# Transposing k and q by DMA and holding attention back, in a kernel that fuses attention with a two-layer MLP

## The chip, the cores and the metric

The kernel runs on one core of a Trainium2 chip. The core has a matrix engine (TensorE, PE in the profile, with its weight loads as PEld), a vector engine (DVE), an activation engine (ACT), GpSimd (POOL) and SyncE (SP), which here issues all DMAs. The metric is the device time of one execution in microseconds: 277.5 us before, the median of three runs (277.43 to 278.24).

## The reference

Eight batches of attention with 8 heads, 576 positions and 64 values per head. First 32 packed queries p per head attend over k and v; then the positions q attend over the 32 packed results. The output, 4608 tokens of 512 values, goes through an MLP with 2048 hidden values and a swish with a slope for each hidden value. All inputs and the output are float32.

```python
p_packed = sm_attn(p, k, v)                 # softmax(p k^T / 8) v
out = sm_attn(q, p_packed, p_packed)        # softmax(q pp^T / 8) pp
x = out.transpose(0, 2, 1, 3).reshape(4608, 512)
h = x @ w_in
g = h * (1 / (1 + exp(-beta * h)))
return g @ w_out
```

## The kernel before

The kernel works in bf16 with float32 sums. It goes batch by batch through four stages. Each head's 576 positions are split into a main part of 512 and a remainder of 64.

**Loads.** SP loads k, q and v of a batch as float32 (`plan_loads`, issues at L214 for the main part and L222 for the remainder, two DMAs), POOL casts them into one bf16 tile of 128 x 2304 each (L242, L248; DVE for the main part of batch 0). There is one float32 tile and one bf16 tile for each of k, q and v, so the load of the next batch waits for the cast, and the cast for the last reader of the bf16 tile (`readers`, L258).

**Transposes.** TensorE transposes k and q of each batch: four groups of eight 128x128 blocks (`transpose`, L270, two groups each), and four blocks for the remainders of both (`transpose_rest`, L300). DVE copies the results from PSUM to SBUF (`evacuate`, L277; `evacuate_rest`, L310), into one tile for k (kT, with kTr for the remainder) and one for q (qT).

**Attention.** The first scores `s1` and `s1r` (L332, L348) multiply the transposed k with p; ACT takes the exponentials; `z1` sums them, `pun` multiplies with v (the packing product, L395, tile pp_ps), `pp` normalizes. The second scores `s2` (L430) multiply the transposed q with pp; ACT exponentials, sums `z2`, and on ACT a logarithm and an exponential give the reciprocal; DVE makes the weights A2 (L480). Since the second attention and W1 are both linear in pp, the product of pp and w_in is made first (`fused_w`, L525) and scaled with beta by DVE (`scaled_w`, tile W, L537).

**MLP.** W1 (`h`, L562) multiplies W with A2 in 16 pieces of two matmuls of 512 columns, ACT takes silu into g_main (L570). `hr` does it for the remainder. W2 (`o`, L620) multiplies g_main with w_out: four token groups t of 16 matmuls each (64 a batch), summed in one PSUM bank a group; the remainders of two batches make one more group of 16 (g_rem). DVE copies a group's result to o_sb (three tiles, L629), SP stores it (L637, L641).

**What sets the order.** All this is written as tasks with an engine, an estimated duration, dependencies and a rank (`task`, L190). `Planner.run` (L63) simulates the engines with these durations and emits the instructions of each engine in the order in which the simulated engines start them: a free engine takes the ready task with the lowest rank. W1 of batch b has rank 100b - 300, its attention 100b - 30 and above, loads 100b, W2 100b + 260: so W2 fills in where nothing else is ready. On the chip each engine runs its instructions in this fixed order and waits for semaphores. PSUM is planned as three rings: two banks for h, two for o, four ("att") for the rest. ACT has one table of functions for exp and ln and another for silu; the planner decides when it changes (L109 to L118). Before 36 us it fills a free TensorE with dummy matmuls (L120, warm_ps).

W1 of batch b waits for the whole of W2 of batch b-2 (`oldg`, L599), since g_main has two buffers; A2 and W of batch b wait for W1 of batch b-2.

Of the kernel before, what the change touches and what calls it, by code (L numbers as in the profile page):

```python
# [29 lines left out]
LAND_US = 2.0  # L30
WARM_UNTIL = 36.0
WN = 1


class Task:

    __slots__ = ("engine", "us", "fn", "deps", "rank", "takes", "count", "ends", "table", "end", "slot", "left", "ready", "users", "key")

    def __init__(self, engine, us, fn, deps, rank, takes, count, ends, table):
# [4 lines left out]
        self.left, self.ready = 0, 0.0  # L46


class Planner:
# [8 lines left out]
    def add(self, engine, us, fn, deps=(), rank=0, takes=None, count=1, ends=(), table=None):  # L58
        t = Task(engine, us, fn, [d for d in deps if d is not None], rank, takes, count, ends, table)
        self.tasks.append(t)  # L60
        return t

    def run(self):  # L63
# [72 lines left out]
class Kernel:  # L136
# [128 lines left out]
    def plan_attention(self, b):  # L265
# [10 lines left out]

        def evacuate(x, i, engine):  # L277
            if i == 0:
                st[b, x, "T"] = self.tr.tile(
                    [128, NC, S if x == "q" else SM], bf16, tag=f"{x}T", name=f"{x}T"  # L280
                )
            self.copy[engine](  # L282
                st[b, x, "T"][:, 2 * i : 2 * i + 2, 0:SM],
                st[b, x, "ps", i][:].rearrange("p (c n) -> p c n", c=2),
            )

        for x in "kq":
            old = [("s1", b - 1, i) for i in range(2)] if x == "k" else [("s2", b - 1, i) for i in range(2)]
            for i in range(2):
                tr = self.task(  # L290
                    ("tr", b, x, i), "PE", 0.45, lambda x=x, i=i: transpose(x, i),
# [16 lines left out]
                    )  # L308

        def evacuate_rest(x):  # L310
            ps = st[b, "r", "ps"]
            if x == "k":
                st[b, "kr"] = t = self.tr.tile([128, 2, 128], bf16, tag="kTr", name="kTr")
                nc.vector.tensor_copy(t[:], ps[:, 0:256].rearrange("p (u n) -> p u n", u=2))
            else:
                nc.vector.tensor_copy(
                    st[b, "q", "T"][:, :, SM:S].rearrange("p (g u) n -> p u g n", u=2),
                    ps[:, 256:512].rearrange("p (u g n) -> p u g n", u=2, g=2),
                )

        trr = self.task(
            ("trr", b), "PE", 0.24, transpose_rest,
            [("cast", b, "k", 2), ("cast", b, "q", 2), ("s1r", b - 1), ("T", b, "q", 1)], rank + 1, takes="att",
        )
        rk = self.task(("rk", b), "DVE", 0.28, lambda: evacuate_rest("k"), [trr], rank + 1)
        self.task(("rq", b), "DVE", 0.28, lambda: evacuate_rest("q"), [trr, rk], rank + 1, ends=[trr])


        E = lambda: self.E1T[b % 2]
# [18 lines left out]
        def scores1_rest():  # L348
            st[b, "s1r"] = ps = self.att("s1r_ps")
            for u in range(2):  # L350
                self.mm(
                    ps[:, 0:256].rearrange("p (g u e) -> p u g e", g=2, u=2)[:, u],
                    st[b, "kr"][:, u, :],
                    pT().rearrange("p (g u) e -> p u g e", u=2)[:, u],
                )

# [70 lines left out]
        self.task(("pp", b), "DVE", 0.6, normalize1, [i1, pun], rank + 4, ends=[pun])  # L427


        def scores2(name, lo, hi):  # L430
            for r in range(2):
                st[b, name, r] = self.att(name + "_ps")
            for c in range(NC):
                for r in range(2):
                    self.mm(
                        st[b, name, r][32 * c : 32 * c + 32, 0 : hi - lo],
                        st[b, "pp"][64 * r : 64 * r + 64, c, :],
                        st[b, "q", "T"][64 * r : 64 * r + 64, c, lo:hi],
                        pos=(64 * r, 32 * c),
                    )  # L440

# [38 lines left out]
        def weights2(i):  # L480
# [17 lines left out]
        s2r = self.task(  # L498
            ("s2", b, 1), "PE", 0.14, lambda: scores2("s2r", SM, S),
            [("pp", b), ("rq", b), s2] + oldE, rank + 5, takes="att", count=2,  # L500
        )
        e2r = [
# [366 lines left out]
```

## Time and profile before

| what | value |
|---|---|
| median of three runs | 277.5 us |
| the profiled execution, as a whole | 278.71 us |
| its span, first to last instruction | 276.8 us |
| mean granted TensorE clock | 0.991 |
| HBM read and written | 37.23 MB and 9.44 MB |
| changes of ACT's table | 32, 41.1 us |
| DVE waiting for W2's results before copying them | 83.2 us |

The profile was taken from one execution. Times within it start at its first instruction. A group row gives line, engine, operation, output and inputs with shapes, count, then busy time and mean ns of one, then idle time of the engine just before them and what ended most of it. Matmuls are pipelined, their ends are modelled and overlap the next ones, so the distance between starts says how long an instruction holds the engine in a full queue. In rows of the timeline the brackets hold the idle time before and what ended it. The DMA queue of SP appears as SPq.

### The profile page before, as it was taken

What the parts mean: (1) busy time and instruction counts of PE and PEld (TensorE: products, weight loads), DVE (VectorE), ACT (ScalarE), POOL (GpSimd) and SP (SyncE); (2) the same over time, 40 slices, a digit from 0 to 9 for tenths busy, and PEclk for the clock granted to TensorE, in tenths of its full rate; (3) what the DMA queues carried; (4) which work ended last, traced back from release to release, by engine and by line L of the source; (5) the groups of instructions that cost most, each with busy time, mean ns of one, the idle gap of its engine ahead of it and who ended that gap; (6) DMA issues with size and microseconds to landing.
All of it is one profiled execution on the core that took longest, in us unless ns stands there. A gap on an engine that the chain in (4) does not pass through costs nothing.

```text
span 276.8 us, 5707 instructions
## 1 busy us (share of the span) xinstructions
PE 260.0 (94%) x2394; PEld 138.7 (50%) x2394; DVE 131.8 (48%) x232; ACT 173.0 (62%) x296; POOL 60.6 (22%) x58
## 2 busy tenths in 40 slices
PE   4998687979999999999999999999999999999993
PEld 4995254535555444654365434564355444454441
DVE  6645744798239635823752374224681373021120
ACT  1457458695988798588867984678648875630000
POOL 4107633060444630063005400044000000000000
PEclk9999998899999999999999999999999999999999
DMA  6999999958999999208920793000200110111112
GB/s 208 294 344 357 315 288 370 341 175 232 290 295 313 276 284 287 57 0 252 334 83 0 225 336 108 22 18 38 78 38 15 49 54 38 38 40 76 76 76 76
DMA packets 47736, 47.02 MB, mean 170 GB/s; under 512 B 14288, under 2 KB 38880, under 8 KB 47712
## 3 DMA queue, kind: packets, MB, share of 16 engines
q1 hardware_dynamic: 47712, 46.68, 56.2%
q8 instruction: 18, 0.29, 0.5%
q14 instruction: 6, 0.05, 0.1%
HBM read 37.23 MB, written 9.44 MB: 169 GB/s over the span
## 4 chain that ended last, share of the span: by engine, by line
PE 86%; DVE 5%; DMA 3%; ACT 2%; SPq 1%; issue 0%; POOL 0%; POOLq 0%; DVEq 0%
PE o_ps L167 45%; PE h_ps L167 18%; PE w_ps L167 3%; DMA w_out<-in_moe_w_out_dram 3%; PE hr_ps L167 3%; PE kT_ps L172 2%; PE qT_ps L172 2%; PE z_ps L167 2%; PE warm_ps L167 2%; PE s_ps L167 2%; DVE A2T L483 2%; PE pp_ps L167 2%; PE brow_ps L167 2%; SPq L222 1%; DVE W_bf L542 1%; DVE identr L672 1%
## 5 line engine op out<-in xcount | busy, mean ns | idle before, releaser
L167 PE MATMUL o_ps<-w_out_bf,g_main 128*128 128x512 bf16 x512 | 125.6, 381 | 3.8 <-DVE w_out_bf L791 2.0
L573 ACT ACTIVATE g_main<-h_ps 128x512 bf16<-128x512 f32 x128 | 71.2, 595 | 46.5 <-PE h_ps L167 46.0
L167 PEld LDWEIGHTS <-g_main 128*128 128x128 bf16 x512 | 46.9, 98 | 57.2 <-issue 8.5
L167 PE MATMUL h_ps<-A2T,W_bf 128*128 128x512 bf16 x256 | 69.9, 381 | 1.2 <-DVE W_bf L542 1.1
L631 DVE COPY o_sb<-o_ps 128x512 f32<-128x512 f32 x36 | 24.8, 690 | 83.3 <-PE o_ps L167 83.2
L167 PEld LDWEIGHTS <-W_bf 128*128 128x128 bf16 x512 | 32.0, 98 | 27.4 <-issue 3.9
L542 DVE TENSOR_TENSOR W_bf<-w_ps,beta_bc 128x512 bf16<-128x512 f32 x64 | 40.7, 681 | 7.2 <-PE w_ps L167 7.1
L182 ACT ACT_TABLE_LOAD x32 | 41.1, 1283 | 1.3 <-PEq L853 0.7
L242 POOL CAST k_bf<-k 128x2048 bf16<-128x2048 f32 x7 | 13.4, 1912 | 82.9 <-PE remT_ps L172 66.7
L483 DVE TENSOR_TENSOR A2T<-E2T,rz 128x512 bf16<-128x512 bf16 (+1 forms) x24 | 17.4, 753 | 6.1 <-ACT rz L478 6.0
L242 POOL CAST v_bf<-v 128x2048 bf16<-128x2048 f32 x7 | 13.5, 1932 | 23.6 <-DMA v<-in_v_dram 11.9
L167 PE MATMUL warm_ps<-identr 128*128 128x128 bf16 x177 | 14.8, 235 | 3.7 <-DVE bones L676 3.7
L167 PE MATMUL o_ps<-w_out_bf,g_rem 128*128 128x512 bf16 x64 | 15.6, 379 | 0.0
L167 PEld LDWEIGHTS <-identr 128*128 128x128 bf16 x177 | 12.3, 106 | 6.3 <-DVE bones L676 3.7
L242 POOL CAST q_bf<-q 128x2048 bf16<-128x2048 f32 x7 | 13.3, 1897 | 4.2 <-DMA q<-in_q_dram 2.3
L282 DVE COPY kT<-kT_ps 128x1024 bf16<-128x1024 bf16 x15 | 10.0, 683 | 8.3 <-PE kT_ps L172 8.3
L167 PE MATMUL w_ps<-w_in_bf,pp 64*32 64x512 bf16 x256 | 13.0, 386 | 0.5 <-POOL w_in_bf L781 0.5
L478 ACT ACTIVATE rz<-rz 128x512 f32<-128x512 f32 (+1 forms) x24 | 12.6, 524 | 0.8
L393 DVE RECIPROCAL rz<-z_ps 128x128 f32<-128x128 f32 x8 | 7.6, 955 | 10.5 <-PE z_ps L167 10.5
L167 PEld LDWEIGHTS <-pp 64*32 64x32 bf16 x384 | 4.9, 88 | 15.4 <-issue 11.0
L593 ACT ACTIVATE g_rem<-hr_ps 128x512 bf16<-128x512 f32 x16 | 9.3, 595 | 4.8 <-PE hr_ps L167 4.8
L172 PEld LDWEIGHTS <-k_bf 128*128 128x128 bf16 x144 | 9.4, 98 | 5.4 <-POOL k_bf L242 1.4
(67 smaller groups left out, 209.0 us busy)
## 6 DMA issues: line engine op xcount, KB each, us to landing
out_dram<-o_sb SPq DMA_DIRECT2D x32, 256.0 KB, 2.4
k<-in_k_dram SPq DMA_DIRECT2D x7, 1024.0 KB, 8.6
q<-in_q_dram SPq DMA_DIRECT2D x7, 1024.0 KB, 9.1
v<-in_v_dram SPq DMA_DIRECT2D x7, 1024.0 KB, 8.5
w_in<-in_moe_w_in_dram SPq DMA_DIRECT2D x4, 1024.0 KB, 10.2
w_out<-in_moe_w_out_dram SPq DMA_DIRECT2D x4, 1024.0 KB, 9.5
k<-in_k_dram SPq DMA_DIRECT2D x2, 512.0 KB, 5.7
k<-in_k_dram SPq DMA_DIRECT2D x16, 64.0 KB, 6.6
```

The lines of the kernel that those rows point to most:

```text
L167: return self.nc.tensor.matmul(out, lhsT, rhs, start=start, stop=stop, tile_position=pos, skip_group_check=True)
L172: return self.nc.tensor.matmul(out, in_, ident, is_transpose=True, skip_group_check=True)
L182: self.nc.scalar.preload_act_table_set(SETS[mode])
L242: self.copy[engine](o[:, 0:2048].rearrange("p (t h d) -> p h t d", t=4, h=8)[:, h], t[:, 0:2048].rearrange("p (h t d) -> p h t d", h=8, t= ...
L282: self.copy[engine](st[b, x, "T"][:, 2 * i : 2 * i + 2, 0:SM], st[b, x, "ps", i][:].rearrange("p (c n) -> p c n", c=2),)
L393: nc.vector.reciprocal(rz[:], st[b, "z1"][:, 0:128])
L478: nc.scalar.activation(rz, rz, AF.Exp, scale=-1.0)
L483: nc.vector.tensor_tensor(part(st[b, "A2"], i), part(st[b, "E2"], i), part(st[b, "rz2"], i), ALU.mult)
L542: nc.vector.tensor_tensor(st[b, "W"][:, r, cols], st[b, "w", m][:], self.beta_bc[:, cols], ALU.mult)
L573: nc.scalar.activation(st[b, "g"][:, ft, :], st[b, "h", ft][:], AF.Silu)
L593: nc.scalar.activation(st[b // 2, "gr"][:, 8 * half : 8 * half + 8, o : o + 64], st[b, "hr", half][:].rearrange("p (f n) -> p f n", f=8), ...
L631: nc.vector.tensor_copy(o[:], st[b, "o", t][:])
```

## The change

For batches 2 to 7 the transposes on TensorE, their PSUM tiles and the copies by DVE are gone; one transposing DMA for k and one for q, each SBUF to SBUF from the whole bf16 tile of 128 x 2304, are issued by SP. Batches 0 and 1 keep TensorE's transposes. kT and qT are now both 128 x 18 x 128 (block, position in block), the remainders in blocks 16 and 17; the copies of batches 0 and 1 and the matmuls that read the tiles are indexed accordingly. As before there is one tile for each, so k's transfer waits for its three casts and for the first scores of the batch before, q's for its casts and the second scores of the batch before. The planner counts 3.0 us on SP for a transfer, 2.0 us of landing as for a load, and 2.0 us more (LAG).

The first scores of batch b, which start its attention, get a dependency on W2 of batch b-2, group 1, last pair (its 32nd matmul of 64), and the second scores one on group 2, last pair (the 48th).

In the planner a task can carry a lag that is added to the time at which its users are ready. And where ACT changes its table, the task of lowest rank that asked for the change is now started at once, with the table's time added; before, only the table was changed, and the choice was made anew after it.

```diff
+LAG = 2.0
+PACE = (1, 15, 2, 15)
+PE_BATCHES = 2
...
-        def start(t):
+        def start(t, extra=0.0):
...
-            t.end = now + t.us
+            t.end = now + t.us + extra
...
-                u.ready = max(u.ready, t.end + (0.0 if u.engine == t.engine else land))
+                u.ready = max(u.ready, t.end + (0.0 if u.engine == t.engine else land) + u.lag)
...
                         self.switch(mode)
-                        free[e] = now + TABLE_US
+                        start(min(other, key=lambda t: t.rank), TABLE_US)
...
         def evacuate(x, i, engine):
             if i == 0:
-                st[b, x, "T"] = self.tr.tile(
-                    [128, NC, S if x == "q" else SM], bf16, tag=f"{x}T", name=f"{x}T"
-                )
+                st[b, x, "T"] = self.tr.tile([128, 18, 128], bf16, tag=f"{x}T", name=f"{x}T")
...
+        def transpose_dma(x):
+            st[b, x, "T"] = t = self.tr.tile([128, 18, 128], bf16, tag=f"{x}T", name=f"{x}T")
+            nc.sync.dma_start_transpose(t[:], st[b, x][:])
 
         for x in "kq":
             old = [("s1", b - 1, i) for i in range(2)] if x == "k" else [("s2", b - 1, i) for i in range(2)]
+            if b >= PE_BATCHES:
+                d = self.task(
+                    ("tr", b, x, 0), "SP", 3.0, lambda x=x: transpose_dma(x),
+                    [("cast", b, x, i) for i in range(3)] + old + [("s1r" if x == "k" else "none", b - 1)], rank, lag=LAG,
+                )
+                for i in range(2):
+                    self.tk["T", b, x, i] = self.tk["tr", b, x, i] = d
+                self.tk["r" + x, b] = d
+                continue
...
-        trr = self.task(
-            ("trr", b), "PE", 0.24, transpose_rest,
...
+        if b < PE_BATCHES:
+            trr = self.task(
+                ("trr", b), "PE", 0.24, transpose_rest,
...
-                    o, a = 256 * t + 64 * c, 128 * (2 * i + t)
-                    self.mm(ps[:, o : o + 64], kT[:, c, a : a + 128], pT()[:, c, :])
+                    o, a = 256 * t + 64 * c, 4 * (2 * i + t)
+                    self.mm(ps[:, o : o + 64], kT[:, a + c, :], pT()[:, c, :])
...
-        s1r = self.task(("s1r", b), "PE", 0.12, scores1_rest, [("rk", b), ("pT",)] + old, rank + 2, takes="att")
+        s1r = self.task(("s1r", b), "PE", 0.12, scores1_rest, [("rk", b), ("pT",), ("o", b - 2, PACE[0], PACE[1])] + old, rank + 2, takes="att")
...
-                        st[b, "q", "T"][64 * r : 64 * r + 64, c, lo:hi],
+                        q[h, 16 + c % 2, g : g + 64] if rest else q[h, c : 16 : NC, :],
...
-            ("s2", b, 0), "PE", 0.3, lambda: scores2("s2", 0, SM), [("pp", b)] + tq + oldE, rank + 5, takes="att", count=2
+            ("s2", b, 0), "PE", 0.3, lambda: scores2("s2", False), [("pp", b), ("o", b - 2, PACE[2], PACE[3])] + tq + oldE, rank + 5, takes="att", count=2
```

More of the change, by code (lines that the diff above doesn't have):

```diff
@@ L32, with __init__ @@
 WN = 1
+LAG = 2.0
+PACE = (1, 15, 2, 15)
+PE_BATCHES = 2
 class Task:
-    __slots__ = ("engine", "us", "fn", "deps", "rank", "takes", "count", "ends", "table", "end", "slot", "left", "ready", "users", "key")
-    def __init__(self, engine, us, fn, deps, rank, takes, count, ends, table):
+    __slots__ = ("engine", "us", "fn", "deps", "rank", "takes", "count", "ends", "table", "end", "slot", "left", "ready", "users", "key", "lag")
+    def __init__(self, engine, us, fn, deps, rank, takes, count, ends, table, lag):
         self.engine, self.us, self.fn, self.deps, self.rank = engine, us, fn, deps, rank
@@ L46, in __init__ @@
         self.left, self.ready = 0, 0.0
+        self.lag = lag
 class Planner:
@@ L56, in __init__, with add @@
         self.switch, self.filler = switch, filler
-    def add(self, engine, us, fn, deps=(), rank=0, takes=None, count=1, ends=(), table=None):
-        t = Task(engine, us, fn, [d for d in deps if d is not None], rank, takes, count, ends, table)
+    def add(self, engine, us, fn, deps=(), rank=0, takes=None, count=1, ends=(), table=None, lag=0.0):
+        t = Task(engine, us, fn, [d for d in deps if d is not None], rank, takes, count, ends, table, lag)
         self.tasks.append(t)
@@ L310, in evacuate_rest @@
         def evacuate_rest(x):
[L311 to L319, printed above, removed]
-        trr = self.task(
-            ("trr", b), "PE", 0.24, transpose_rest,
[L323 to L326, printed above, removed]
+            o = 0 if x == "k" else 256
+            nc.vector.tensor_copy(
+                st[b, x, "T"][:, 16:18], st[b, "r", "ps"][:, o : o + 256].rearrange("p (u n) -> p u n", u=2)
+            )
+        if b < PE_BATCHES:
+            trr = self.task(
+                ("trr", b), "PE", 0.24, transpose_rest,
+                [("cast", b, "k", 2), ("cast", b, "q", 2), ("s1r", b - 1), ("T", b, "q", 1)], rank + 1, takes="att",
+            )
+            rk = self.task(("rk", b), "DVE", 0.28, lambda: evacuate_rest("k"), [trr], rank + 1)
+            self.task(("rq", b), "DVE", 0.28, lambda: evacuate_rest("q"), [trr, rk], rank + 1, ends=[trr])
         E = lambda: self.E1T[b % 2]
@@ L427, in plan_attention, with scores2 @@
         self.task(("pp", b), "DVE", 0.6, normalize1, [i1, pun], rank + 4, ends=[pun])
-        def scores2(name, lo, hi):
+        def scores2(name, rest):
+            n = SR if rest else SM
             for r in range(2):
@@ L434, in scores2 @@
                 for r in range(2):
+                    h, g = slice(64 * r, 64 * r + 64), 64 * (c // 2)
+                    q = st[b, "q", "T"]
                     self.mm(
-                        st[b, name, r][32 * c : 32 * c + 32, 0 : hi - lo],
-                        st[b, "pp"][64 * r : 64 * r + 64, c, :],
-                        st[b, "q", "T"][64 * r : 64 * r + 64, c, lo:hi],
+                        st[b, name, r][32 * c : 32 * c + 32, 0:n],
+                        st[b, "pp"][h, c, :],
+                        q[h, 16 + c % 2, g : g + 64] if rest else q[h, c : 16 : NC, :],
                         pos=(64 * r, 32 * c),
@@ L498, in plan_attention @@
         s2r = self.task(
-            ("s2", b, 1), "PE", 0.14, lambda: scores2("s2r", SM, S),
+            ("s2", b, 1), "PE", 0.14, lambda: scores2("s2r", True),
             [("pp", b), ("rq", b), s2] + oldE, rank + 5, takes="att", count=2,
```

6 lines of the change are left out of this document (3 added, 3 removed).

## The prediction

> **What bounds the kernel now.** I read the page first: shares, slices, chain.
>
> ```profile
> span 276.8 us, 5707 instructions
> PE 260.0 (94%) x2394; PEld 138.7 (50%) x2394; DVE 131.8 (48%) x232; ACT 173.0 (62%) x296; POOL 60.6 (22%) x58
> PE   4998687979999999999999999999999999999993
> DMA  6999999958999999208920793000200110111112
> PE 86%; DVE 5%; DMA 3%; ACT 2%; SPq 1%; issue 0%; POOL 0%; POOLq 0%; DVEq 0%
> ```
>
> TensorE is busy for 94% of the span and makes up 86% of the chain that ended last. But busy time of a matmul is a modelled, overlapping time, and a share over the span mixes stages. So next the busy time by stretches (columns: stretch, its length, then busy time and count of PE, PEld, DVE, ACT, POOL, then granted clock, DMA share, GB/s).
>
> ```profile
> 36.00:61.00 25.00, 20.40 (x195) 10.73 (x191) 15.67 (x30) 19.76 (x32) 8.46 (x7) 0.93 0.95 306
> 61.00:117.00 56.00, 56.00 (x566) 28.93 (x565) 33.29 (x58) 44.33 (x76) 17.54 (x16) 1.00 0.92 254
> 117.00:209.00 92.00, 92.00 (x833) 46.27 (x831) 42.89 (x75) 65.20 (x115) 20.01 (x18) 1.00 0.38 115
> 59.71:272.10 212.39, 212.38 (x1826) 105.22 (x1825) 94.68 (x163) 137.53 (x237) 38.71 (x34) 1.00 0.45 134
> ```
>
> There are two stages. Until 59.7 us TensorE has gaps beside a DMA that is 95% busy: that stage waits for data. From 59.71 to 272.10 us TensorE has one hundredth of a microsecond without work. In that stage what leaves TensorE's queue leaves the time, as long as nothing takes the place. ACT is the next engine: from 61 to 209 us it is busy 44.33 + 65.20 = 109.5 of 148 us.
>
> **What leaves TensorE.** The timeline of TensorE (start, length, instructions, idle before) shows the two large gaps of the first stage, the first transposes of batch 2, and all transposes of batch 5.
>
> ```profile
> 45.32 1.74 PE L167 MATMUL o_ps<-w_out_bf,g_main 128*128 128x512 bf16 x6 [2.04 <-DVE w_out_bf L791]
> 59.71 1.46 PE L167 MATMUL o_ps<-w_out_bf,g_main 128*128 128x512 bf16 x6 [1.71 <-DVE o_sb L631]
> 61.00 0.61 PE L172 MATMUL kT_ps<-identr,k_bf 128*128 128x128 bf16 x8
> ...
> 142.96 1.06 PE L172 MATMUL kT_ps<-identr,k_bf 128*128 128x128 bf16 x16
> 143.85 1.03 PE L167 MATMUL h_ps<-A2T,W_bf 128*128 128x512 bf16 x4
> 144.72 1.06 PE L172 MATMUL qT_ps<-identr,q_bf 128*128 128x128 bf16 x16
> 145.61 1.03 PE L167 MATMUL h_ps<-A2T,W_bf 128*128 128x512 bf16 x4
> ...
> 148.20 0.27 PE L172 MATMUL remT_ps<-identr,k_bf 128*128 128x128 bf16 x2
> 148.31 0.28 PE L172 MATMUL remT_ps<-identr,q_bf 128*128 128x128 bf16 x2
> 148.43 0.59 PE L167 MATMUL o_ps<-w_out_bf,g_main 128*128 128x512 bf16 x2
> ```
>
> The lengths overlap, so I take the distance from start to start: 16 transposes hold the queue from 142.96 to 143.85, 0.89 us, 16 more from 144.72 to 145.61, and the four of the remainder from 148.20 to 148.43, 0.23 us. That is 2.01 us a batch, and 6 x 2.01 = **12.06 us** for batches 2 to 7. Those of batch 2 start at 61.00, so all six lie in the full stage. The Trainium skill ("VectorE: DVE Perf Modes", section "The three transpose paths") gives 390 ns for one 128x128 transpose on TensorE; by it the 216 removed ones would free 84 us (an estimate). The trace has 0.89 / 16 = 56 ns each in a full queue, and the trace decides.
>
> **What leaves DVE and the PSUM ring.** The groups and one wait:
>
> ```profile
> L282 DVE COPY kT<-kT_ps 128x1024 bf16<-128x1024 bf16 x15 | 10.0, 683 | 8.3 <-PE kT_ps L172 8.3
> L314 DVE COPY kTr<-remT_ps 128x256 bf16<-128x256 bf16 x8 | 2.3, 288 | 9.7 <-PE remT_ps L172 9.7
> ACT g_main L573 <- PE h_ps L167: 46.0, 64, 2.6
> ```
>
> Each batch loses four copies of 0.68 us and two of 0.29 us on DVE, 3.3 us, and five uses of the four-slot ring "att". DVE is busy 94.7 of 212 us in the second stage, so I count this at nothing: TensorE hides it. ACT waits 46 us for W1's results, so it has room when TensorE comes sooner: with 12 us less, 109.5 us of work stand against about 136 us. The planner's edit at a table switch makes the task that asked for the switch the first one after it; ACT is off the path, so nothing either (if ACT were on it, one needless pair of table loads would be some 2.6 us). Batches 0 and 1 keep their transposes; their copies write the same elements in another order, nothing. The matmuls read the new layout in the same counts and lengths, nothing.
>
> **What is moved: the hold.** The first scores of batch b wait for the 32nd matmul of W2 of batch b-2, the second scores for the 48th. Columns as above, cut to instructions that read g_main; the stretches end where the first scores of batches 2, 3, 5 and 7 start, and the number behind PE counts W2's main matmuls so far.
>
> ```profile
> 0.00:70.82 70.82, 12.91 (x48) 4.48 (x48) 14.49 (x25) 0.98 0.96 292
> 0.00:95.06 95.06, 25.84 (x98) 9.04 (x98) 22.52 (x39) 0.98 0.99 293
> 0.00:149.29 149.29, 51.38 (x198) 17.89 (x198) 40.59 (x72) 0.99 0.85 250
> 0.00:209.76 209.76, 84.05 (x330) 29.61 (x330) 58.07 (x104) 0.99 0.70 206
> 170.18 1.03 PE L167 MATMUL h_ps<-A2T,W_bf 128*128 128x512 bf16 x4
> 167.67 1.29 DVE L542 TENSOR_TENSOR W_bf<-w_ps,beta_bc 128x512 bf16<-128x512 f32 x2 [0.44 <-PE w_ps L167]
> ```
>
> Batch 2 needs 32 and has 48; batch 3 needs 96 and has 98: no change. Batch 5 needs 224 and has 198, batch 7 needs 352 and has 330: there attention moves back behind 26 and 22 matmuls, some 5 us of TensorE's work. The work is the same, in another order, so in itself it costs nothing. What is queued behind the held scores on TensorE is everything later in its order, but the planner puts W2 in between. The danger is the other side: from the first scores at 149.29 to the last scaled W at 168.96 the chain takes 19.7 us, its matmuls and W2's second half included, and W1 of the next batch starts behind it, at 170.18. With 26 matmuls gone from this cover, up to 26 x 0.216 = 5.6 us of it lie open (four matmuls take 0.87 us, 143.85 to 144.72), unless the planner fills in W2 of batch b-1, whose inputs are complete when W1 of that batch is. It can, by rank and by its dependencies, so I count nothing.
>
> **What is added: twelve transposing DMAs on SP's queue.** The trace has none, so I bound one from the rows for DMA: the queue (packets, MB, share of 16 engines), loads of k (KB, us to landing), two kinds of issue on SP (start and us of one; ns min/median/max of 16), the last cast of k of batch 2, the second scores of batch 7 and the stretch up to them.
>
> ```profile
> q1 hardware_dynamic: 47712, 46.68, 56.2%
> k<-in_k_dram SPq DMA_DIRECT2D x7, 1024.0 KB, 8.6
> 124.20 0.37 SPq L214 DMA_DIRECT2D k<-in_k_dram  x1
> L222 SPq DMA_DIRECT2D k<-in_k_dram x16: 607/708/2922, 2.7 to 154.8; - x16
> 58.34 0.86 POOL L248 CAST k_bf<-k 128x256 bf16<-128x256 f32 x1
> ...
> 216.70 0.41 PE L167 MATMUL s_ps<-qT,pp 64*32 64x512 bf16 x8
> 59.20:216.70 157.50, 156.99 (x1475) 79.71 (x1474) 80.70 (x141) 117.99 (x203) 38.71 (x34) 1.00 0.56 160
> ```
>
> One moves 128 x 2304 x 2 bytes, 0.59 MB. Below: at the queue's own mean while busy (46.68 MB in 0.562 x 276.8 = 155.6 us, 300 GB/s) it holds the 16 engines 2.0 us, and 0.37 us of issue as for a plain load. Above: in rows of 256 bytes it is 2304 pieces; the queue's mean packet costs 155.6 x 16 / 47712 = 52 ns of one engine, so 2304 of them hold all 16 for 7.5 us; and 256 such rows of a 64 KB load take SP 0.61 us at least, so 2304 take 5.5 us. A transfer below nothing is excluded. I take **3 us** of the engines, nearer the byte rate, because the source is contiguous along each partition; both ends are kept. The skill gives two prices. "DMA: Bandwidth & Descriptors", section "Latency and other measured facts", has 261 GB/s, 2.3 us for one (an estimate), inside my bounds. "VectorE: DVE Perf Modes" has 1309 ns for 128x128, 23.6 us for 18 such blocks (an estimate), far outside; no run here shows either.
>
> Is 3 us hidden? From 59.2 us (k of batch 2 is cast) to 216.7 us the DMA is 56% busy, 88 us; 69 us are free, 59 once the stretch is 10 us shorter. Twelve at 3 us are 36: hidden in the sum, up to 59 / 12 = 4.9 us each. In time, too: k's transfer of batch b waits for its cast and for the first scores of batch b-1, q's for the second scores of b-1, and these lie a batch before the use, 24 us by the rows of 70.82 and 95.06; a plain load lands in 8.6. Queued behind a waiting transfer on SP are later loads and the stores of results. Three o_sb tiles and two banks of o_ps cover a late store for two tiles or more; a tile of 16 matmuls takes at least 16 x 0.216 = 3.5 us. POOL's cast of the next k and q will be released by the transfer instead of TensorE, so loads start sooner; from 117 us on they find a DMA that is 38% busy.
>
> **Batch 2 is the exception**, since its data arrive just in time (POOL casts, then TensorE):
>
> ```profile
> 63.90 0.40 POOL L248 CAST q_bf<-q 128x256 bf16<-128x256 f32 x1 [2.17 <-DMA q<-in_q_dram]
> 70.78 1.90 POOL L242 CAST v_bf<-v 128x2048 bf16<-128x2048 f32 x1 [6.47 <-DMA v<-in_v_dram]
> 72.61 0.40 POOL L248 CAST v_bf<-v 128x256 bf16<-128x256 f32 x1
> 90.47 1.90 POOL L242 CAST k_bf<-k 128x2048 bf16<-128x2048 f32 x1 [3.77 <-PE remT_ps L172]
> ...
> 75.78 0.76 PE L167 MATMUL pp_ps<-E1T,v_bf 128*128 128x64 bf16 x20
> ```
>
> v is cast at 73.0 us and used at 75.8: 2.8 us of slack. Without 2.0 us of transposes TensorE is there at 73.8, slack 0.8. If k's transposing DMA (3 us) runs ahead of v's load in the full queue, v is late by 3 - 0.8 = 2.2 us. I take **2 us lost**; bounds 0 (it runs behind v) and 5.2 us (q's runs ahead as well). From batch 4 on (90.47) POOL waits for TensorE to free a buffer, not for DMA, so later batches have slack.
>
> **The sum.** 276.8 - 12.06 + 2.0 = 266.7 us of span. The profiled execution took 278.71 us, 1.2 more than the median 277.5; I take the difference from the median: 277.5 - 10.06 = **267.4 us**.
>
> **Rivals.** (a) Better: v of batch 2 is not late, and the new order closes part of the 2.04 and 1.71 us gaps: 277.5 - 12.06 = 265.4, down to 261.7 with both gaps closed. For it: the second gap is a matter of order. Against: the first is a late w_out. (b) Late data: both transfers are ahead of v (277.5 - 12.06 + 5.2 = 270.6), and stores held up on SP cost two more gaps like that of 1.71 us: up to 274. For it: the queue is 92% busy there. Against: from batch 4 on the loads run ahead. (c) No gain: another engine takes the place, 277.5. Against: ACT at 80%. (d) The hold drains TensorE: if W2 of batch b-1 doesn't fill, 5.6 us in each of batches 4 to 7, 22 us, 290; it is slower than before from 10 / 4 = 2.5 us each. Against: the rank lets W2 in whenever nothing else is ready. (e) **Slower by the transfers:** at 7.5 us each the 16 engines have 88 + 90 = 178 us of work in a stretch of 147.5 us; TensorE waits the 30 us, 298 us. It decides from 4.9 us each, and is slower than before from 4.9 + 10 / 12 = 5.7 us. Against: the byte rate. By the 1309 ns of "VectorE: DVE Perf Modes" in the Trainium skill this rival would hold, with 88 + 12 x 23.6 = 371 us of transfers in the same stretch and some 490 us (an estimate).
>
> **How the numbers follow.** Forecast 0.54 (265.4 to 270.6), (a) 0.13, (b) 0.13, (c) 0.05, (d) 0.06, (e) 0.09. Forecast, (a) and (b) hold 0.80, so the range is 262 to 274. Faster by over 0.3% (what a measurement here can tell from no change): 0.80; within: 0.05; slower: (d) and (e), 0.15.
>
> **What would show it.** Right: no transposes on TensorE behind 60 us, TensorE without gaps from there to the end, a span of about 267, and a gap of 2 us before the packing product of batch 2. The transfers should land well before the scores that read them. Wrong: gaps of TensorE that end with a transposing DMA or with a store's buffer (e), gaps before W1 that end with A2 or W (d), or a transfer that holds the 16 engines over 5 us.

## The result, and the profile after

The changed kernel took 267.7 us (median of four runs, 266.5 to 275.6) beside 277.5 us for the kernel before: a ratio of 0.963, with an interval from 0.959 to 0.966. Two later sets of runs on other chips gave 270.0 and 269.3 us, ratios of 0.974 (0.964 to 0.984) and 0.973 (0.967 to 0.978). The change makes the kernel about 3% faster, near the 267.4 us forecast.

The profiled execution of the first set was a disturbed one (275.6 us, the highest of its set), and so were those of e2, e4 and e10 below; none of them is read for times. What follows is an execution of the same changed kernel from a later set, 268.8 us as a whole. Its page, the lines that answer to those of before (span; busy time, share and count of each engine; slices of TensorE and the DMA; the chain that ended last):

```profile
span 266.9 us, 5267 instructions
PE 247.1 (93%) x2178; PEld 126.0 (47%) x2178; DVE 110.2 (41%) x196; ACT 174.9 (66%) x298; POOL 59.7 (22%) x58
PE   4978877999796999999999999999999999999992
DMA  6999999999999999989999999936621111111112
PE 73%; DMA 10%; SPq 5%; ACT 5%; DVE 4%; POOL 1%; issue 1%; POOLq 0%; DVEq 0%
```

TensorE has 216 instructions fewer and DVE 36 fewer, as the change says. The DMA is now full to slice 26 of 40 (173 us) instead of slice 16, and in the chain the DMA and SP's queue have gone from 4% to 15% together: v's loads alone are 7%, 18.4 us, of which 10.5 us lead to v of batch 2 (the steps that start at 58.81 and 71.28). Busy time by stretches of the changed kernel (columns as before: stretch, length, PE, PEld, DVE, ACT, POOL, granted clock, DMA share, GB/s):

```profile
36.00:61.00 25.00, 22.29 (x220) 11.19 (x219) 15.77 (x33) 21.32 (x35) 7.70 (x7) 1.00 1.05 321
61.00:117.00 56.00, 51.90 (x451) 24.37 (x450) 23.70 (x41) 41.62 (x73) 16.73 (x15) 0.97 1.04 239
117.00:209.00 92.00, 92.00 (x789) 43.85 (x788) 34.48 (x60) 70.05 (x121) 20.54 (x19) 1.00 0.80 201
85.38:262.20 176.82, 176.70 (x1408) 83.40 (x1406) 63.17 (x106) 118.19 (x203) 30.70 (x28) 0.99 0.66 163
```

From 85.4 us to 262.2 us, nearly the end of its work, TensorE is practically without a gap again (0.1 us), with the freed time gone. Between 61 and 117 us it is not: 4.1 us of 56 are idle. The timeline of TensorE shows where, with the two gaps of the first stage above them (start, length, instructions, in brackets the idle time before and what ended it):

```profile
44.79 1.63 PE L171 MATMUL o_ps<-w_out_bf,g_main 128*128 128x512 bf16 x6 [1.59 <-DVE w_out_bf L805]
56.41 2.32 PE L171 MATMUL o_ps<-w_out_bf,g_main 128*128 128x512 bf16 x10 [0.17 <-DVE o_sb L645]
...
69.03 0.28 PE L171 MATMUL s1r_ps<-pT,kT 128*128 128x128 bf16 x2 [1.42 <-DMA kT<-k_bf]
...
74.29 0.64 PE L171 MATMUL pp_ps<-E1T,v_bf 128*128 128x64 bf16 x16 [0.43 <-POOL v_bf L252]
...
81.77 0.37 PE L171 MATMUL w_ps<-w_in_bf,pp 64*32 64x512 bf16 x1 [0.36 <-ACT rz L481]
82.60 0.41 PE L171 MATMUL w_ps<-w_in_bf,pp 64*32 64x512 bf16 x8 [0.45 <-ACT rz L483]
84.22 0.41 PE L171 MATMUL w_ps<-w_in_bf,pp 64*32 64x512 bf16 x7 [1.22 <-DVE W_bf L556]
84.85 0.74 PE L171 MATMUL h_ps<-A2T,W_bf 128*128 128x512 bf16 x2 [0.21 <-ACT g_main L587]
```

Batch 2 pays three times: 1.42 us for k's transfer, 0.43 us for the remainder of v, and 2.24 us at its product W (0.36 + 0.45 + 1.22 + 0.21). At that last place the kernel before had the 32 main transposes of batch 3 and more of W2 around the pieces of W; here nothing is left that is ready. Rows of the kernel before:

```profile
84.81 0.41 PE L167 MATMUL w_ps<-w_in_bf,pp 64*32 64x512 bf16 x8
85.16 0.62 PE L172 MATMUL qT_ps<-identr,q_bf 128*128 128x128 bf16 x8
85.61 1.46 PE L167 MATMUL o_ps<-w_out_bf,g_main 128*128 128x512 bf16 x6
```

The account of the spans: 12.06 us of transposes out, 4.1 us of new gaps in batch 2, 1.71 - 0.17 = 1.5 us and 2.04 - 1.59 = 0.45 us of gaps closed in the first stage: 9.9 us, and 276.8 - 266.9 is 9.9. It comes out because one more term cancels: in both executions the granted clock (third number from the right) fell to half for some 3.3 us soon after a gap, in the kernel before after the 2.04 us gap, in the changed one after the gaps at W. The first row is the kernel before, the second the changed one:

```profile
46.80:50.10 3.30, 3.30 (x35) 2.12 (x35) 2.44 (x6) 1.04 (x2) 0.00 (x0) 0.50 0.95 353
85.38:88.60 3.22, 3.22 (x43) 2.14 (x42) 1.87 (x4) 1.19 (x2) 1.85 (x3) 0.50 1.30 197
```

That is about 1.6 us lost in each (an estimate: half of the stretch), so batch 2's gaps cost some 5.7 us in this execution. (The two executions are from different chips, so the agreement to a tenth is luck.)

The DMA queue of the changed kernel (packets, MB, share of 16 engines) and the transfers (count, median us from issue to landing), and SP's issues around batch 2 (start and length):

```profile
q1 hardware_dynamic: 75744, 53.76, 76.0%
kT<-k_bf SPq DMA_TRANSPOSE x6, 8.7
qT<-q_bf SPq DMA_TRANSPOSE x6, 4.8
```

```profile
58.81 0.40 SPq L218 DMA_DIRECT2D v<-in_v_dram  x1
59.39 7.55 SPq L291 DMA_TRANSPOSE kT<-k_bf  x1
...
67.74 2.81 SPq L291 DMA_TRANSPOSE qT<-q_bf  x1
70.60 1.29 SPq L226 DMA_DIRECT2D v<-in_v_dram  x2
```

The queue's busy time went from 155.6 us to 0.760 x 266.9 = 202.8 us: **3.9 us of all 16 engines for one transfer**, by the time of its packets (4.1 us by a0's trace; the second twelve of e5, below, come to 3.2). There are 28032 more packets, 2336 a transfer: it does go in pieces of about 256 bytes. An issue takes SP 2.8 us at best and 7.55 us for k of batch 2, right behind the main load of v, and both transfers of batch 2 stand ahead of the remainder of v.

### The profile page after: what moved, and what is told of

It is laid out like the page before. It is cut to its first block, busy times and chain, and to the rows that moved or that the text cites. A ratio compares the mean times of both kernels' runs of the same rounds, so it can differ in the third digit from the quotient of the medians.

```text
span 273.7 us, 5267 instructions
## 1 busy us (share of the span) xinstructions
PE 251.0 (92%) x2178; PEld 127.3 (47%) x2178; DVE 117.1 (43%) x196; ACT 174.9 (64%) x298; POOL 61.2 (22%) x58
## 4 chain that ended last, share of the span: by engine, by line
PE 72%; DMA 11%; DVE 10%; SPq 3%; issue 2%; ACT 1%; POOL 0%; POOLq 0%; DVEq 0%
PE o_ps L171 39%; PE h_ps L171 16%; DMA kT<-k_bf 4%; DVE A2T L497 4%; DMA q<-in_q_dram 4%; DMA w_out<-in_moe_w_out_dram 3%; DVE W_bf L556 3%; PE w_ps L171 3%; PE hr_ps L171 2%; SPq L226 2%; PE warm_ps L171 2%; PE s_ps L171 2%; PE z_ps L171 2%; PE brow_ps L171 2%; PE pp_ps L171 2%
## 5 line engine op out<-in xcount | busy, mean ns | idle before, releaser
L171 PE MATMUL o_ps<-w_out_bf,g_main 128*128 128x512 bf16 x512 | 129.5, 386 | 2.1 <-DVE w_out_bf L805 2.0
L171 PEld LDWEIGHTS <-g_main 128*128 128x128 bf16 x512 | 48.0, 99 | 61.1 <-issue 11.1
L171 PE MATMUL h_ps<-A2T,W_bf 128*128 128x512 bf16 x256 | 69.2, 382 | 1.4 <-DVE W_bf L556 1.4
L171 PEld LDWEIGHTS <-W_bf 128*128 128x128 bf16 x512 | 33.1, 99 | 30.8 <-issue 2.7
L497 DVE TENSOR_TENSOR A2T<-E2T,rz 128x512 bf16<-128x512 bf16 (+1 forms) x24 | 20.7, 895 | 9.3 <-ACT rz L492 9.2
L171 PE MATMUL w_ps<-w_in_bf,pp 64*32 64x512 bf16 x256 | 13.6, 393 | 4.5 <-DVE W_bf L556 3.4
L481 ACT ACTIVATE rz<-z_ps 128x512 f32<-128x512 f32 x16 | 9.4, 588 | 3.1 <-PE z_ps L171 3.1
L459 ACT ACTIVATE E2T<-s_ps 128x512 bf16<-128x512 f32 x16 | 8.7, 594 | 2.7 <-PE s2r_ps L171 2.6
```

Of the source, the lines that this page charges most:

```text
L171: return self.nc.tensor.matmul(out, lhsT, rhs, start=start, stop=stop, tile_position=pos, skip_group_check=True)
L459: nc.scalar.activation(st[b, "E2"][:, i, 0:SM], st[b, "s2", i][:], AF.Exp, scale=SCALE)
L481: nc.scalar.activation(rz[:, i, 0:SM], ps[:], AF.Ln)
L497: nc.vector.tensor_tensor(part(st[b, "A2"], i), part(st[b, "E2"], i), part(st[b, "rz2"], i), ALU.mult)
```

## The experiments

Each row was measured beside the kernel before on the same chip; rows of one group share a chip. Ratios are to the kernel before, with the interval of 95%.

| run | what differs from the changed kernel | median us | before | ratio |
|---|---|---|---|---|
| a0_after | nothing | 270.0 | 277.75 | 0.974 (0.964 to 0.984) |
| e1_no_hold | no hold | 286.4 | | 1.031 (1.023 to 1.039) |
| e2_hold_only | no transfers | 277.5 | | 0.997 (0.992 to 1.002) |
| e3_batch2_on_pe | batch 2 transposed on TensorE | 267.4 | | 0.964 (0.956 to 0.971) |
| e4_old_switch | planner's old table switch | 269.7 | 276.61 | 0.973 (0.967 to 0.978) |
| e5_double | every transfer twice | 289.3 | | 1.045 (1.037 to 1.053) |
| e6_lag8 | LAG 8 instead of 2 | 271.5 | | 0.982 (0.975 to 0.989) |
| e7_no_hold_lag12 | no hold, LAG 12 | 294.7 | | 1.064 (1.059 to 1.070) |
| e10_no_hold_few_loads | no hold, no loads after batch 2 | 279.0 | 277.31 | 1.005 (1.001 to 1.009) |
| e11_half_hold | hold half as deep | 270.9 | | 0.977 (0.971 to 0.983) |
| a1_after | nothing | 269.3 | | 0.973 (0.967 to 0.978) |
| e12_batch2_on_pe | as e3 | 267.2 | | 0.965 (0.960 to 0.969) |

**The two parts, each alone.** The changed kernel once more, without the hold, with the hold alone (`PE_BATCHES = 8`, so that TensorE transposes all batches; the tile layout and the planner's edit stay), and with batch 2 left to TensorE (`PE_BATCHES = 3`).

```diff
-        s1r = self.task(("s1r", b), "PE", 0.12, scores1_rest, [("rk", b), ("pT",), ("o", b - 2, PACE[0], PACE[1])] + old, rank + 2, takes="att")
+        s1r = self.task(("s1r", b), "PE", 0.12, scores1_rest, [("rk", b), ("pT",)] + old, rank + 2, takes="att")
...
-            ("s2", b, 0), "PE", 0.3, lambda: scores2("s2", False), [("pp", b), ("o", b - 2, PACE[2], PACE[3])] + tq + oldE, rank + 5, takes="att", count=2
+            ("s2", b, 0), "PE", 0.3, lambda: scores2("s2", False), [("pp", b)] + tq + oldE, rank + 5, takes="att", count=2
```

> The changed kernel as it is, to look at an undisturbed profile. Theory: span near 265.5 us, total 266.5 to 268.5; one gap of TensorE of 2 to 3 us before the first scores of batch 2 (end of the transfer of k), little else behind 62 us. Rival: the missing 2 us against 12.06 are spread over waits in later batches; then several gaps, each under 1 us, behind 100 us.

> The two dependencies on W2 of batch b-2 are taken out, the transposing DMAs stay. Theory (the hold only reorders): 266.5 to 268.5 us, as the changed kernel. Rival (the hold keeps W2 back as cover and so brings part of the gain): 270 us or more, with gaps of TensorE in the later batches or at the end. Second rival (the hold costs): under 266 us.

> All batches transpose on TensorE, the hold, the tile layout and the planner's edits stay. Theory (the gain is the 12 us of transposes alone): 276.5 to 278.5 us, as before. Rival (the hold or the planner's edit brings part of it): under 275 us. Second rival (the hold opens gaps that the missing transposes hid): over 280 us.

> Batch 2 too transposes on TensorE, batches 3 to 7 by DMA. Theory (batch 2 loses about what it frees, since k, q and v come late behind the transfers): 2.0 us of work come back, the gap of 2 to 3 us before the first scores of batch 2 goes: 266 to 268.5 us, no change within a microsecond. Rival (batch 2 frees its 2 us in full and the loss lies elsewhere): 269 to 270 us. Second rival (batch 2 costs more than it frees): under 266 us.

Without the hold the change does not gain 3% but loses 3%. The hold alone does nothing that can be told from zero, though it does change the order (table below). In a0's trace batch 2 pays at the three places named above, 4.4 us, where one gap of 2 to 3 us was expected. So the gain belongs to neither part, only to both: the hold decides 16 us, by which the prediction's "I count nothing" missed. In e1, TensorE's busy time by stretches, its largest wait for data (total, times, longest), and the place of the longest, with the first scores of batch 5 before it:

```profile
61.00:117.00 56.00, 47.27 (x416) 21.79 (x415) 22.98 (x40) 40.53 (x70) 16.59 (x15) 0.97 1.05 238
117.00:209.00 92.00, 84.22 (x702) 39.71 (x701) 35.23 (x54) 64.00 (x109) 21.26 (x19) 0.94 0.75 190
```

```profile
PE s1r_ps L171 <- DMA kT<-k_bf: 10.9, 4, 5.6
```

```profile
139.48 0.28 PE L171 MATMUL s1r_ps<-pT,kT 128*128 128x128 bf16 x2
...
155.69 0.39 PE L171 MATMUL s1r_ps<-pT,kT 128*128 128x128 bf16 x2 [5.56 <-DMA kT<-k_bf]
```

Between 61 and 209 us TensorE is idle for 16.5 us, 12.4 more than in the changed kernel, and the lower clock costs up to 5 us more (0.03 x 47.27 + 0.06 x 84.22 us, less 1.6 in the changed kernel; an estimate). The two spans are 17.4 us apart. What led to the longest wait, on SP and POOL (the two transfers of batch 5, then k of batch 6: the issue of its load, its two casts, the issue of its transfer):

```profile
125.47 7.08 SPq L291 DMA_TRANSPOSE kT<-k_bf  x1
133.28 2.95 SPq L291 DMA_TRANSPOSE qT<-q_bf  x1
138.26 0.60 SPq L218 DMA_DIRECT2D k<-in_k_dram  x1
145.12 1.90 POOL L246 CAST k_bf<-k 128x2048 bf16<-128x2048 f32 x1 [4.32 <-DMA k<-in_k_dram]
146.96 0.40 POOL L252 CAST k_bf<-k 128x256 bf16<-128x256 f32 x1
147.39 6.31 SPq L291 DMA_TRANSPOSE kT<-k_bf  x1
```

TensorE reaches the first scores of batch 6 at 155.69 - 5.56 = 150.1 us, 10.6 us after those of batch 5. kT has one buffer, so its transfer for batch 6 cannot begin before batch 5's scores. But they are not what it waited for last: it is issued at 147.39, as soon as k's last cast is done (147.36), 7.9 us after the start of those scores. The cast waited for k's load, and the load was issued only at 138.26, though the cast of batch 5 had freed its float32 tile at 125.2: the issues of batch 5's two transfers, 10.0 us, stood ahead of it on SP. From its issue to the first scores the transfer takes 8.3 us: 16.2 us between the two scores against 10.6. The forecast had 24 us between the two. That was the spacing of the old order. TensorE's instructions show how the order depends on the hold: W2's main matmuls that stand before the first scores of each batch,

| | batch 2 | 3 | 4 | 5 | 6 | 7 |
|---|---|---|---|---|---|---|
| before | 48 | 98 | 136 | 198 | 262 | 330 |
| changed | 58 | 96 | 160 | 224 | 288 | 352 |
| e1, no hold | 58 | 90 | 128 | 192 | 212 | 320 |
| e2, hold alone | 52 | 98 | 160 | 224 | 288 | 352 |
| e11, half hold | 58 | 92 | 144 | 208 | 272 | 336 |
| e7, no hold, LAG 12 | 76 | 128 | 152 | 196 | 256 | 320 |

In the changed kernel batches 4 to 7 sit exactly on the hold (160, 224, 288, 352), 64 apart. Without it the planner places batch 6 only 20 matmuls behind batch 5, since its model counts 3 us on SP for a transfer and lets kT arrive 7 us after its issue begins. In the planner, taking away only the hold of the second scores leaves every engine's order as it is; so it is the first one that works.

e3 answers the other question. Its account comes below, with e12.

**Is it late data alone?** If the planner's model of the transfer is too quick, a longer lag should serve as well as the hold. e6 and e7 set it (`LAG = 8.0` with the hold, `LAG = 12.0` without). e5 doubles the transfer's price, with the hold:

```diff
         def transpose_dma(x):
             st[b, x, "T"] = t = self.tr.tile([128, 18, 128], bf16, tag=f"{x}T", name=f"{x}T")
             nc.sync.dma_start_transpose(t[:], st[b, x][:])
+            nc.sync.dma_start_transpose(self.spare[:], st[b, x][:])
```

e4 puts back the planner's old behaviour at a change of ACT's table:

```diff
-                        start(min(other, key=lambda t: t.rank), TABLE_US)
+                        free[e] = now + TABLE_US
```

> No hold, and the planner counts 12 us instead of 2 for the extra landing of a transfer, so that it places the first scores 10 us later. Theory (without the hold the planner puts the first scores right behind the planned landing, the real one is later, and TensorE, which works in order, stands still; any slack will do): the gaps that end with a transfer of k, 10.9 us without the hold, fall under 3 us, 267 to 272 us. Rival (attention running ahead uses up the cover by W2, whatever the landing): 278 us or more, with gaps that end with DVE or ACT. Second rival (the DMA has no room for the transfers): gaps that end with a transfer stay above 8 us, 282 us or more.

> Each transposing DMA is issued twice, the second time into a tile that nobody reads: twelve more of the same transfers. One holds the 16 engines 4.2 us by the queue's share (50.5 us more in the profile of the changed kernel, over twelve). Theory (room for them is nearly used up: the DMA was busy for 136 of the 148 us from 61 to 209): 50 us more of transfers for 12 us of room, TensorE waits for data in most batches, 290 to 310 us. Rival (the hold hides their time, only latency counts): under 275 us.

> The changed kernel with 8 us instead of 2 for the planner's extra landing of a transfer; the hold stays. With it the planner also sets v of batch 2 ahead of both transfers on SP. Theory (1.53 us on the transfer of k and 0.64 us on v of batch 2 are a matter of the planned landing): both gaps under 0.5 us in all, the gaps at W of batch 2 (2.25 us) stay, 1 to 3 us faster than the changed kernel on the same chip: 266 to 269 us. Rival (batch 2 waits for data whatever the order): the gaps move to another wait of batch 2, time as the changed kernel, 269 to 271 us.

> The planner's edit at a change of ACT's table is undone, transfers and hold stay. Theory (ACT is off the path): within 1.5 us of the changed kernel on the same chip, 267 to 271 us. Rival (the edit avoids needless changes of the table and so is a part of the gain): 273 us or more, with more than 34 table loads.

The theory that any slack will do fell: e7 is the slowest kernel of all. Its stretches and TensorE's three largest waits behind the start (total, times, longest):

```profile
61.00:117.00 56.00, 48.48 (x382) 21.53 (x380) 19.41 (x33) 32.64 (x59) 17.66 (x16) 0.94 1.03 253
117.00:209.00 92.00, 80.58 (x642) 35.77 (x642) 29.60 (x50) 71.13 (x114) 20.09 (x18) 0.89 0.69 169
```

```profile
PE s1r_ps L171 <- DMA kT<-k_bf: 5.9, 3, 3.0
PE z2r_ps L171 <- ACT E2T L462: 5.8, 3, 2.5
PE h_ps L171 <- ACT g_main L587: 4.9, 4, 1.7
```

The waits for k fell from 10.9 to 5.9 us, as the lag means them to. But TensorE now waits 10.7 us for ACT, in two groups. The clock falls too: between 61 and 209 us TensorE is idle for 18.9 us (changed kernel: 4.1), and by the granted clocks of 0.94 and 0.89 it loses another 11.8 us (0.06 x 48.48 + 0.11 x 80.58; changed kernel: 1.6), an estimate that makes up 25 of the 26.3 us between the two spans. The lag delays a batch's attention in the plan without tying it to W2, and attention of two batches falls together: between the first scores of batches 4 and 5 stand 44 matmuls of W2 and 10 of W1 (before: 62 and 36). Attention needs ACT at every step, and the only work of TensorE that ACT delivered long before is W2. So two things can make up the loss without a hold, data that come late and attention that crowds ACT, each with a lower clock after its gaps, and spreading attention over W2 works against both. Their shares are another question.

e4 shows no effect of the switch edit (0.973 with and without it, each known to about 0.6%); ACT loads a table 34 times in both, so what a needless change would cost is not tested. e6, a longer lag on top of the hold, gains nothing where 1 to 3 us were expected: 0.982 (0.975 to 0.989) beside 0.973. In its trace the wait for v of batch 2 is gone and the gaps at W stay, but that for k's transfer has grown from 1.42 to 2.48 us.

e5 shows how much room the transfers have left. Its queue, stretches and largest wait:

```profile
q1 hardware_dynamic: 103776, 60.84, 83.9%
```

```profile
61.00:117.00 56.00, 43.83 (x365) 20.09 (x364) 20.83 (x34) 35.88 (x62) 12.48 (x12) 0.91 1.04 234
117.00:209.00 92.00, 84.24 (x716) 39.74 (x715) 29.59 (x50) 61.74 (x108) 25.00 (x22) 0.98 1.06 245
```

```profile
PE pp_ps L171 <- POOL v_bf L252: 7.6, 2, 6.0
```

The time is just under the 290 us that were expected at least. Twelve more transfers take the queue to 0.839 x 287.0 = 240.8 us, 38 us more, 3.2 us each, and the DMA is full to 209 us. The wait that grows most is for a plain load, v, that stands behind the transfers. The time rises by 7.2% of the kernel before, 20 us (0.973 to 1.045). The changed kernel is near that edge: 0.80 of the DMA's time between 117 and 209 us is already taken. e5 doubles the issues on SP as well as the work of the DMA engines, so it does not tell which of the two runs out first.

**How much of the loss is late data?** e10 takes the hold away, and with it the loads of k, q and v after batch 2, so that the casts of batches 3 to 7 read batch 2's float32 tiles again; TensorE, ACT, DVE and POOL run e1's instructions in e1's order. e11 makes the hold half as deep, `PACE = (0, 15, 1, 15)`.

```diff
+                if b > 2:
+                    self.t[b, x, "32"] = self.t[2, x, "32"]
+                    return
```

> The kernel without the hold, whose TensorE, ACT, DVE and POOL run the same instructions in the same order, but the loads of k, q and v of batches 3 to 7 are left out: their casts read batch 2's float32 tiles again. Only the DMA has less to do. Theory (without the hold the first scores are placed earlier than the DMA can bring their data; TensorE stands still and its clock falls): the waits on transfers of k, 10.9 us without the hold, go, and with them the low clock: 264 to 271 us. Rival (the order itself is bad: attention runs so far ahead of W1 and W2 that TensorE waits for ACT and DVE): 278 us or more.

> The hold one group of W2 earlier: first scores of batch b wait for 16 instead of 32 matmuls of W2 of batch b-2, second scores for 32 instead of 48. Theory (the hold works by the time that it gives the data): 16 matmuls, 3.5 us, less in batches 4 to 7, some wait on a transfer of k comes back, 269 to 276 us, between the two. Rival (what counts is only that attention doesn't run more than one batch ahead): as the changed kernel, within 1.5 us.

> The changed kernel again, beside the next one on the same chip: 267 to 271 us.

> Batch 2 too transposes on TensorE, again, beside the changed kernel. Theory (batch 2's transfers cost as much as they free, 4.4 us of gaps against 2.0 us of work): 1 to 3 us faster than the changed kernel, 266 to 269 us. Rival (the difference on the first chip was scatter): within 1 us of the changed kernel.

With early loads, e1's order goes from 1.031 to 1.005: 2.6%, about 7 us, are what the loads, and with them most of SP's queue, cost there. Another 3.2%, about 9 us, lie between that and the changed kernel at 0.973, and stay with e1's order (by the intervals, each of the two is known to about 1% of the time). So late loads are not the whole loss: 1.005 x 277.31 = 278.7 us is what the rival said (278 or more), and the theory's 264 to 271 us did not come. How the 9 us divide between waits for ACT, a lower clock after gaps and what is left of late transfers stays open. Half the hold (0.977) can't be told from the whole (0.973), since the intervals overlap. Its trace points the expected way: TensorE waits 3.6 us for k's transfers, beside 1.4 with the whole hold and 10.9 without.

**Batch 2.** e12 repeats e3 with the changed kernel on the same chip: 267.2 beside 269.3 us, and e3 267.4 beside 270.0. Of the versions on each of these two chips it is the fastest; the intervals of each pair overlap, but both pairs point the same way, and the trace shows why. Stretches of the changed kernel and, in the second fence, of e12, around batch 2, and what stands at the place of W in e12:

```profile
61.00:85.38 24.38, 20.28 (x171) 8.93 (x170) 9.40 (x18) 18.26 (x32) 6.58 (x7) 1.00 1.01 248
```

```profile
61.00:85.38 24.38, 24.15 (x233) 11.92 (x231) 12.66 (x23) 19.35 (x34) 9.65 (x9) 1.00 1.00 248
```

```profile
81.10 0.41 PE L171 MATMUL w_ps<-w_in_bf,pp 64*32 64x512 bf16 x8
81.44 1.90 PE L171 MATMUL o_ps<-w_out_bf,g_main 128*128 128x512 bf16 x8
83.27 0.41 PE L171 MATMUL w_ps<-w_in_bf,pp 64*32 64x512 bf16 x8
```

The transposes of batch 2 cost TensorE 2.0 us, but with them go 4.10 - 0.23 = 3.9 us of gaps: k needs no transfer in the full queue, v's remainder is loaded straight behind its main part, and the order leaves eight matmuls of W2 for the place where W waited. Net 1.9 us; the two pairs of medians give 2.0 and 2.6. Behind its gaps the changed kernel also lost some 1.6 us to the clock in this execution, which e12 did not; in a0, with the same gaps, the clock stayed at 1.00, so this differs from one execution to the next.

## Why the prediction was right, step by step

**What the transposes are worth** held: 12.06 us by the distances between starts. The account of the spans needs this number, and e12, which gives 2 us of it back and gains 3.9, fits it too.

**DVE, the PSUM ring and the table switch at nothing** held. e4 shows it for the switch, with no change of the ratio that can be told; for the rest there is only the account, which leaves no place for them.

**ACT is not the next bound**, in this order. It is busy 41.62 + 70.05 = 111.7 of 148 us between 61 and 209 us, and TensorE has no gap there but batch 2's. In e7's order TensorE waits 10.7 us for it, at the same total of work. So the forecast's argument from ACT's share was not safe; what protects TensorE is how ACT's work is spread.

**The hold at nothing: this step failed.** The text weighed only what the hold could uncover, by its own count of W2 matmuls, and found cover; there it was right, since rival (d), a drained TensorE, did not come. It compared the held order with the order of before, though. The order that counts is the one the planner would make of the transfers without a hold, and that one is e1's, at 1.031. By itself the hold is indeed worth nothing (e2), in this kernel it is worth 16 us (e1 beside a0).

**"In time, too"** failed with it, as an argument: 24 us between a transfer's release and its use came from rows of the old order, and the transposes' removal lets the planner make a new one. It holds in the changed kernel, where the first scores of batches 2 and 3 start at 69.03 and 91.19 us and later batches keep 64 matmuls of W2 between them. It holds because of the hold. The text also had the loads start sooner. In e1 the transfers' issues on SP held k's load back, and what released the transfer of batch 6 was k's cast at 147.36 us, not the scores of batch 5 that began at 139.48.

**The transfer's price** was a size off: 3 us taken, 3.9 measured, within the bounds of 2.0 and 7.5. The byte rate was the nearer row, but the pieces of 256 bytes, which the upper bound stood on, are there; whether they make the difference no run shows. By 3.9 us, twelve transfers hold the DMA 47 of the 59 us that were free, and the edge that the text put at 4.9 us each is near: e5, with 3.9 + 3.2 = 7.1 us for each pair, lost 20 us and is slower than before, as rival (e) said for anything above 5.7. By the Trainium skill ("VectorE: DVE Perf Modes", section "The three transpose paths"), 1309 ns for a block, this would have been 23.6 us (an estimate); here 18 blocks hold the engines 3.9 us, and the measurement decides.

**Batch 2 at 2 us** had half the size, and its mechanism, a late v, is a tenth of the loss. Both transfers did run ahead of v's remainder, but v was late by 0.43 us only, where the text named a gap of 2 us as a sign. The text did not price the transfer of k itself, which stands between the last cast and the first scores of batch 2 with no batch in between (1.42 us), nor the place at W, where the transposes of batch 3 had been cover (2.24 us): the loss was 4.1 us.

**The rest of the sum** was made up by a piece of rival (a): the gap of 1.71 us before W2 closed to 0.17 us with the new order. Twice the loss in batch 2 and the gaps closed in the first stage nearly cancel, and so do the falls of the clock in the two executions, which the text did not have. A span of 266.9 beside 266.7 is therefore luck in its last two microseconds; the 12 us of transposes are not. Rival (b), late data at several places, holds for batch 2 alone; no store held TensorE up later.

## What to carry to other kernels

Where instructions come from a planner, price a change against the order that it will make, not the order in the trace: taking work off the bottleneck can move what remains together, and a transfer that was timed well in the old order comes late. Where loads and transfers share a queue, a transfer also delays the next loads, and these the next transfer. A dependency that paces one stage by another's progress can be worth nothing alone and decide the whole in company, so try both parts of a change apart. Leave the batch whose data arrive just in time on the engine that has them: moving it into the full queue cost twice what it freed.

## What the runs showed of the hardware

A gap of TensorE can cost more than its length, because the granted clock may fall after it. Behind the gap of 5.56 us in e1, the stretch from 155.69 on ran at half the clock; behind a gap of 2.76 us in the same kernel nothing fell. Stretches of e1 behind its gaps (the granted clock is the third number from the right):

```profile
114.44:118.57 4.13, 4.13 (x34) 2.06 (x35) 0.00 (x0) 3.59 (x7) 0.02 (x1) 1.00 0.88 173
...
155.69:163.62 7.93, 6.86 (x57) 4.13 (x58) 1.54 (x3) 5.67 (x11) 2.38 (x3) 0.50 0.92 229
```

The same for e7, behind gaps of 2.97 us (ended at 78.51) and 2.00 us (ended at 102.09):

```profile
79.10:84.33 5.23, 5.23 (x22) 1.86 (x18) 0.69 (x1) 1.36 (x4) 2.26 (x3) 0.67 0.64 125
102.09:103.11 1.02, 1.02 (x20) 0.79 (x21) 0.00 (x0) 0.66 (x3) 0.92 (x1) 1.00 0.94 262
103.11:107.48 4.37, 4.37 (x13) 1.47 (x11) 0.69 (x1) 3.34 (x5) 1.42 (x3) 0.61 1.12 172
```

After the gap of 2.00 us the clock stays full for a microsecond and then averages 0.61 over 4.37 us, about 4.37 x 0.39 = 1.7 us lost on top of the 2.0. In the changed kernel the gap of 1.42 us (ended at 69.03) had no such effect:

```profile
69.03:73.17 4.14, 4.14 (x36) 2.07 (x36) 0.69 (x1) 3.83 (x8) 0.00 (x0) 1.00 0.89 173
```

But the four gaps at W, 2.24 us in all between 81.4 and 84.85 us and none longer than 1.22, were followed by half the clock from 85.38 to 88.60 us (row in the section on the result). So were those of e1 (0.36, 0.45, 1.22 and 0.22 us; a mean of 0.55 from 85.23 to 89.00), while a0, with the same four gaps as e1, kept 1.00 from 86.72 to 95.00.

The Trainium skill ("TensorE: Matmul & The Clock Gate", section "Why this matters for your kernels") asks for no idle gaps above about 3 us. These rows go below that: 2.00 us were enough once and 2.76 not enough once, and a row of shorter gaps was enough in two executions and not in a third. What decides between them no run here shows.

A transposing transfer of a tile of 128 x 2304 from SBUF to SBUF goes in 2336 packets, holds the 16 engines 3.9 us by the time of its packets, 0.59 MB / 3.9 us = 151 GB/s, and takes SP between 2.8 and 7.6 us to issue (changed kernel). Where SP issues everything, that is time in which no load and no store gets out: in e1 the two transfers of batch 5 kept SP for 10.0 of the 12.8 us before k's load was issued at 138.26.
